# Attention and a soft mixture of experts: score slots of PSUM that share a bank, or have banks of their own

## The chip, the cores and the metric

The kernel runs on one core of one Trainium2 chip. The metric is the device time of one execution in microseconds (us), as the median over several runs. TensorE (PE in the profile) multiplies matrices into PSUM, a memory of 8 banks; a bank holds 512 float32 columns on each of 128 partitions. VectorE (DVE) and ScalarE (ACT) read PSUM, GpSimd (POOL) works on the other on-chip memory alone, and SyncE (SP) issues most DMAs.

## What is computed

Four batches of 12288 queries attend to 768 pooled keys, which are values at the same time. The rows that come out go through a soft mixture of 8 experts with 4 slots each, whose dispatch weights are normalised over all 49152 rows.

```python
kv_pool = kv.reshape(B, H // 4, 4, W // 4, 4, C).mean(axis=(2, 4))
k = v = kv_pool.reshape(B, -1, C) @ w_sr
a = softmax(q @ k.T / sqrt(C))        # 768 keys
x = (a @ v).reshape(B * N, C)
logits = x @ phi                      # 32 slots
d = softmax(logits, axis=0)           # over all rows
slot_out = experts(d.T @ x)           # 8 experts, 4 slots each
return softmax(logits, axis=1) @ slot_out
```

## The kernel before, in words

The attention's output x is never formed. With P the exponentials of a tile of 128 queries, the kernel forms the logits as P times (v phi), and D^T x as (D^T P) v, D being the dispatch weights of the tile.

There are 384 tiles, 12 to a group, 8 groups to a batch, 32 groups in all. For a tile t, the steps and their names in the plan are: `s` (line 384, `qk`), six matmuls that write 768 scores: query high part times key high part (L395), times key low part (L396), query low part times key high part (L397), for each of two pieces; `m` (L401 and L402, VectorE), the row maximum; `e` (L410, ScalarE), the exponential, which frees the scores. For a pair of tiles: `hi` (L417, ScalarE) and `lo` (L421, GpSimd, one per tile), which split half of P into two float16 parts, `pd` (L430, SyncE), a DMA that transposes them, and `tr` (L434, VectorE), which transposes the other half in blocks. There are two buffers for the split parts, so `hi` of a pair waits for the transposes of the pair two before.

For a group, once its 12 tiles are done: `LA` (L464) and `LB` (L476), the logit sums, 48 and 36 matmuls in the program, into four banks; `lev0` and `lev1` (L484 ScalarE, L486 VectorE), which evict two banks each; `lsel` (L492) and `ltr` (L501 to L504), a small product and a transpose; `mmm` and `mred` (L532, L537), which find the running maximum of the logits; `dsub`, `dexp`, `dmul` (L553, L569, L577), which give D; `T0` to `T5` (L592), the product D^T P, 16 matmuls for a pair of tiles; `tacc` (L603), which adds it to `acc`. All of this belongs to the group before, and stands between the score tiles of the next one. For a batch, the keys are formed by `kv_ops`: `kmm` (L277), `khi` (L280) and `klo` (L284), the high and the low part, `umm` (L292), `umax` (L299), `usc` (L308), and the values `vmm`, `vout`.

PSUM is one tile `m` of 8 banks, divided by hand. Score slot A is columns 0 to 767 (bank 0 and half of bank 1), B is 768 to 1535 (the other half of bank 1, and bank 2), C is 1536 to 2303 (bank 3 and half of bank 4). `PIECES` cuts each at the bank's edge, so a slot has one piece of 512 and one of 256 columns, slot B the 256 first. Which tile of a group has which slot stands in `SLOTS`. The logit sums take banks 5, 6, 3 and 4, hence slot C. Small products use bank 5 (sometimes 6), D^T P bank 7, the key products slot C's banks.

Two things set the order. `TAU` gives each step of a group a place, in tiles; `Plan.emit` sorts by it and by what a step depends on, and each engine runs its instructions in this order. The framework then adds waits: where two engines touch the same bank of the tile `m`, the one that is emitted later waits for the one emitted earlier, whichever columns they use.

Of the kernel before, what the change touches and what calls it, by code (L numbers as in the profile page):

```python
# [19 lines left out]
P = 128  # L20
# [3 lines left out]
SLOTS = "ACBACBAABACB"  # L24
# [38 lines left out]
    "T5": 33.921, "dal": 34.589, "tacc": 35.172, "bev": 36.507, "crec28": 37.068, "csub": 38.581, "bacc": 38.859,  # L63
# [33 lines left out]
def attention_then_soft_moe(ctx: ExitStack, tc: tile.TileContext, E, qT, kv0, kvT, w_sr, w_srT, phi, w1, w2, outT, spill):  # L97
# [32 lines left out]
    gp = es.enter_context(tc.tile_pool(name="gp", bufs=3))  # L130
    pm = es.enter_context(tc.tile_pool(name="pm", bufs=1, space=PSUM))

    CAP = {
        "sA": 1, "sB": 1, "sC": 1, "T": 1, "m0": 1, "m1": 1, "p": 13, "pa": 3, "pb": 3, "hl": 2, "q": 3, "qs": 2, "lps": 1, "g": 3,
        "kv": 2, "K": 2, "V": 1, "c": 16, "o0": 1, "o1": 1, "o2": 1, "o3": 1,
# [42 lines left out]
    mt = pm.tile([P, 8, 512], F32, tag="m", name="m")  # L178
    mf = mt.rearrange("p a n -> p (a n)")
    PIECES = {"A": (0, 512, 768), "B": (768, 1024, 1536), "C": (1536, 2048, 2304)}  # L180
    PAIRS = [slice(0, 2), slice(3, 5), slice(6, 8), slice(2, 6, 3)]

    def ss():
        return mt[:, 3:5, :]

    def xs():
        return mt[:, 5, :]

    def slot(t):
        return SLOTS[t % G]  # L190

# [864 lines left out]
```

## Time and profile before

| | us |
|---|---|
| median of 3 runs | 1192.13 (1189.96 to 1200.83) |
| the profiled execution | 1203.68 |
| its span, first to last instruction | 1201.8 |
| TensorE busy | 919.6 (77%) |
| VectorE busy | 786.6 (65%) |
| ScalarE busy | 656.3 (55%) |
| GpSimd busy | 644.2 (54%) |

The first logit sums start at 75.78 us, the last at 1069.59; between them lie 31 periods of a group. In the first 75 us the first batch's keys are loaded, pooled and multiplied; in the last 132 us the experts are computed and 32 blocks of output are written. In the rows of an engine in order of time, the number in brackets at the end is the idle time of that engine just before the instruction, and what ended it.

### The profile page before, as it was taken

What the parts mean: (1) busy time and instruction counts of PE and PEld (TensorE: products, weight loads), DVE (VectorE), ACT (ScalarE), POOL (GpSimd) and SP (SyncE); (2) the same over time, 40 slices, a digit from 0 to 9 for tenths busy, and PEclk for the clock granted to TensorE, in tenths of its full rate; (3) what the DMA queues carried; (4) which work ended last, traced back from release to release, by engine and by line L of the source; (5) the groups of instructions that cost most, each with busy time, mean ns of one, the idle gap of its engine ahead of it and who ended that gap; (6) DMA issues with size and microseconds to landing.
All of it is one profiled execution on the core that took longest, in us unless ns stands there. A gap on an engine that the chain in (4) does not pass through costs nothing. (4 is left out here: it accounts for less than half of the span.)

```text
span 1201.8 us, 26910 instructions
## 1 busy us (share of the span) xinstructions
PE 919.6 (77%) x10436; PEld 605.2 (50%) x10436; DVE 786.6 (65%) x1496; ACT 656.3 (55%) x1244; POOL 644.2 (54%) x774
## 2 busy tenths in 40 slices
PE   2676888878877888788868878887888888876674
PEld 1544555555545555555545555555555555543342
DVE  5464667767765667676756666677666776754764
ACT  1554556666545656666546656665556665631232
POOL 0354556665645666665565656665555665655500
PEclk9788999999998999999989999999999999987755
DMA  7369666867597767766596776675545555575586
GB/s 275 73 122 128 124 133 122 140 128 139 108 119 138 124 136 137 136 118 137 119 128 128 130 130 125 125 119 93 99 90 99 104 105 104 90 211 240 220 355 265
DMA packets 335264, 168.78 MB, mean 140 GB/s; under 512 B 310432, under 2 KB 312736, under 8 KB 335008
## 3 DMA queue, kind: packets, MB, share of 16 engines
q1 hardware_dynamic: 331248, 149.22, 56.5%
q0 software_dynamic: 3456, 17.70, 9.8%
q8 instruction: 82, 1.34, 0.5%
q14 instruction: 46, 0.38, 0.1%
q10 hardware_dynamic: 432, 0.15, 0.0%
HBM read 62.01 MB, written 28.31 MB: 75 GB/s over the span
## 5 line engine op out<-in xcount | busy, mean ns | idle before, releaser
L401 DVE TENSOR_REDUCE nm<-m 128x1 f32<-128x768 f32 x384 | 366.4, 954 | 316.1 <-PE m L397 281.8
L410 ACT ACTIVATE p<-m,nm 128x768 f32<-128x768 f32 x384 | 344.2, 899 | 357.4 <-DVE nm L401 185.1
L421 POOL TENSOR_TENSOR hl<-p,hl 128x384 f16<-128x384 f32 x384 | 346.9, 922 | 287.6 <-ACT hl L417 217.9
L395 PE MATMUL m<-khi,qhi 128*128 128x512 f32 (+1 forms) x768 | 298.8, 389 | 134.9 <-ACT p L410 128.8
L396 PE MATMUL m<-klo,qhi 128*128 128x512 f32 (+1 forms) x768 | 271.0, 353 | 0.0
L397 PE MATMUL m<-khi,qlo 128*128 128x512 f32 (+1 forms) x768 | 270.6, 352 | 0.0
L395 PEld LDWEIGHTS m<-khi,qhi 128*128 128x128 f32 x768 | 152.1, 198 | 228.2 <-ACT p L410 166.6
L592 PE MATMUL m<-p,D 128*32 128x192 f32 x3072 | 166.8, 338 | 44.2 <-DVE acc L603 35.7
L378 POOL TENSOR_TENSOR qlo<-q,qhi 128x512 fp32r<-128x512 f32 x96 | 123.0, 1282 | 129.5 <-ACT qhi L374 126.8
L434 DVE STREAM_TRANSPOSE pa<-p 128x768 f32<-128x768 f32 x192 | 179.1, 958 | 0.0
L417 ACT ACTIVATE hl<-p 128x768 f16<-128x768 f32 x192 | 160.6, 836 | 30.0 <-DMA pb<-hl 30.0
L397 PEld LDWEIGHTS m<-khi,qlo 128*128 128x128 f32 x768 | 153.5, 200 | 18.0
L396 PEld LDWEIGHTS m<-klo,qhi 128*128 128x128 f32 x768 | 153.9, 200 | 14.7 <-issue 0.2
L592 PEld LDWEIGHTS m<-p,D 128*32 128x32 f32 x3072 | 88.2, 112 | 105.6 <-issue 79.5
L464 PE MATMUL m<-pa,vu 32*32 32x384 f32 x3072 | 91.9, 509 | 2.5 <-DVE pa L434 2.5
L410 ACT ACTIVATION_READ_ACCUMULATOR p<-m,nm 128x1 f32 x384 | 74.9, 195 | 0.0
L986 PE MATMUL m<-ct,sl 32*128 32x384 f32 x256 | 51.7, 845 | 24.2 <-DVE ct L980 23.7
L402 DVE TENSOR_SCALAR nm<-nm 128x1 f32<-128x1 f32 x384 | 59.1, 154 | 13.3
L476 PE MATMUL m<-pb,vb 128*32 128x384 f16 x1152 | 54.2, 333 | 10.6 <-DMA pb<-hl 8.1
L464 PEld LDWEIGHTS m<-pa,vu 32*32 32x32 f32 x3072 | 46.3, 105 | 30.1 <-issue 11.0
L374 ACT ACTIVATE qhi<-q 128x512 fp32r<-128x512 f32 x96 | 59.7, 621 | 1.7 <-PE m L396 1.4
L994 ACT ACTIVATE o<-m 128x768 f32<-128x768 f32 x32 | 24.5, 808 | 51.9 <-PE m L986 28.9
(118 smaller groups left out, 693.8 us busy)
## 6 DMA issues: line engine op xcount, KB each, us to landing
q<-qT SPq DMA_DIRECT2D x96, 256.0 KB, 2.7
outT<-o SPq DMA_DIRECT2D x32, 768.0 KB, 4.3
LL<-kvT POOLq DMA_DIRECT2D x21, 768.0 KB, 8.2
raw<-kv SPq DMA_DIRECT2D x8, 768.0 KB, 9.6
pb<-hl SPq DMA_TRANSPOSE x384, 2.8
w_p<-w SPq DMA_DIRECT2D x6, 768.0 KB, 6.6
pa<-w SPq DMA_DIRECT2D x1, 3328.0 KB, 14.3
spill<-LL SPq DMA_DIRECT2D x16, 192.0 KB, 2.1
```

The lines of the kernel that those rows point to most:

```text
L374: nc.scalar.activation(qsp[i][0], src, AF.Copy)
L378: nc.gpsimd.tensor_tensor(out=lo, in0=src, in1=hi.bitcast(F32), op=ALU.subtract)
L395: nc.tensor.matmul(s, hi[:, qc], khi[:, k], start=True, stop=False)
L396: nc.tensor.matmul(s, hi[:, qc], klo[:, k], start=False, stop=False)
L397: nc.tensor.matmul(s, lo[:, qc], khi[:, k], start=False, stop=True)
L401: nc.vector.tensor_reduce(out=NM[t], in_=S[t], axis=X, op=ALU.max, negate=True)
L410: nc.scalar.activation(PP[t // 2][:, t % 2, :], S.pop(t), AF.Exp, bias=NM.pop(t), scale=1.0, accum_out=R[g][:, o : o + 1],)
L417: nc.scalar.activation(HL[k][:, :, 0, :], PP[k][:, :, KA:], AF.Copy)
L421: nc.gpsimd.tensor_tensor(out=hl[:, 1, :], in0=PP[t // 2][:, t % 2, KA:], in1=hl[:, 0, :], op=ALU.subtract)
L434: nc.vector.transpose(out=PA[:, n, :, o : o + 2, :].rearrange("p n a i -> p a n i"), in_=PP[k][:, :, :KA].rearrange("p a (n j) -> p a n j" ...
L464: nc.tensor.matmul(lp(g, c, r), VU[b][rows, kb, :], PA[rows, halves(g), kb, :, :], start=(k == 0), stop=False, skip_group_check=True)
L592: nc.tensor.matmul(d["pst"][c * Q32 : (c + 1) * Q32, :KW], d["D"][:, t, :], pp[:, u, c * KW : (c + 1) * KW], start=(t == 0), stop=(t == G ...
```

## The change

PSUM is allocated anew. A pool `ps` holds three slots of two banks each, taken strictly in turn; a tile of scores takes one and uses 384 columns in each of its two banks. The logit sums of a group take two of these slots (`lq`), one evicted by VectorE, one by ScalarE. The key products, which used slot C's banks, and the products of the experts at the end take slots of the same ring. A tile `m` of two banks is left: bank 0 of it for all small products, bank 1 for D^T P. The six matmuls of a tile write 384 columns each. The maximum and the exponential read two runs of 384. `SLOTS`, `PIECES` and `PAIRS` go, and the table `TAU` is another one, of which two lines are shown.

```diff
-SLOTS = "ACBACBAABACB"
...
-    "s2": -0.107, "m1": -0.08, "e0": 0.0, "ceps11": 0.495, "e1": 0.588, "s3": 0.879, "m2": 0.962, "ceps4": 1.068,
+    "m1": 0.268, "s2": 0.323, "ceps4": 0.44, "ceps0": 0.521, "s3": 0.871, "e1": 0.965, "m2": 0.986, "m3": 1.534,
...
+    ps = es.enter_context(tc.tile_pool(name="ps", bufs=3, space=PSUM))
...
-        "sA": 1, "sB": 1, "sC": 1, "T": 1, "m0": 1, "m1": 1, "p": 13, "pa": 3, "pb": 3, "hl": 2, "q": 3, "qs": 2, "lps": 1, "g": 3,
-        "kv": 2, "K": 2, "V": 1, "c": 16, "o0": 1, "o1": 1, "o2": 1, "o3": 1,
+        "s": 3, "T": 1, "x": 1, "p": 13, "pa": 3, "pb": 3, "hl": 2, "q": 3, "qs": 2, "lps": 1, "g": 3,
+        "kv": 2, "K": 2, "V": 1, "c": 16, "o": 1,
...
-    mt = pm.tile([P, 8, 512], F32, tag="m", name="m")
-    mf = mt.rearrange("p a n -> p (a n)")
-    PIECES = {"A": (0, 512, 768), "B": (768, 1024, 1536), "C": (1536, 2048, 2304)}
-    PAIRS = [slice(0, 2), slice(3, 5), slice(6, 8), slice(2, 6, 3)]
-
-    def ss():
-        return mt[:, 3:5, :]
+    mt = pm.tile([P, 2, 512], F32, tag="m", name="m")
+
+    def ss(name):
+        return ring(ps, "s", [P, 2, 512], name)
 
     def xs():
-        return mt[:, 5, :]
+        return mt[:, 0, :]
...
-            D["pk", b] = ss()
+            D["pk", b] = ss(f"pk_{b}")
...
-        c0, c1, c2 = PIECES[slot(t)]
-        S[t] = mf[:, c0:c2]
-        for a, e in ((c0, c1), (c1, c2)):
-            k = slice(a - c0, e - c0)
-            s = mf[:, a:e]
+        S[t] = ss(f"s_{t}")
+        for h in range(2):
+            k = slice(h * HK, (h + 1) * HK)
+            s = S[t][:, h, :HK]
...
-        nc.vector.tensor_reduce(out=NM[t], in_=S[t], axis=X, op=ALU.max, negate=True)
+        nc.vector.tensor_reduce(out=NM[t], in_=S[t][:, :, :HK], axis=XY, op=ALU.max, negate=True)
...
-            PP[t // 2][:, t % 2, :], S.pop(t), AF.Exp,
+            PP[t // 2][:, t % 2, :].rearrange("p (h n) -> p h n", h=2), S.pop(t)[:, :, :HK], AF.Exp,
...
-            GD[g]["lp"] = [mt[:, k, :LW] for k in (5, 6, 3, 4)]
+            d = GD[g]
+            d["lq"] = [ss(f"lq_{g}_{u}") for u in range(2)]
+            d["lp"] = [d["lq"][r // 2][:, r % 2, :LW] for r in range(NQD)]
...
-        if u == 0:
-            nc.scalar.activation(d["lps"][:, 2:, :], ss()[:, :, :LW], AF.Copy)
+        dst, src = d["lps"][:, 2 * u : 2 * u + 2, :], d["lq"][u][:, :, :LW]
+        if u:
+            nc.scalar.activation(dst, src, AF.Copy)
         else:
-            nc.vector.tensor_copy(d["lps"][:, :2, :], mt[:, 5:7, :LW])
+            nc.vector.tensor_copy(dst, src)
...
-            d["pst"] = mt[:, 7, :]
+            d["pst"] = mt[:, 1, :]
```

Three places of the program where instructions move follow. In these rows a number behind a name tells one tile from another, `nm_146` is the row maximum of score tile 146, and what stands behind "waits" are the semaphores of the engines that the instruction waits for.

The first is ScalarE's queue before, around the exponentials of score tiles 145 to 149, the second to the sixth of group 12; `hl` is the conversion `hi`, `p` the exponentials.

```order
L410 ACTIVATE p_72_4276,r_12_4275<-m_96,nm_145_4272 128x768 [waits DVE_49]
L417 ACTIVATE hl_71_4300<-p_71_4212 128x2x384 [waits DMAHW0_49,DMAHW7_49,Activation_49,Pool_49]
L410 ACTIVATE p_73_4312,r_12_4275<-m_96,nm_146_4297 128x768 [waits DVE_49,PE_49]
L410 ACTIVATE p_73_4312,r_12_4275<-m_96,nm_147_4309 128x768 [waits DVE_49]
L410 ACTIVATE p_74_4338,r_12_4275<-m_96,nm_148_4323 128x768 [waits DVE_49,PE_49]
L417 ACTIVATE hl_72_4341<-p_72_4276 128x2x384 [waits DMAHW2_49,DMAHW3_49,Activation_49,Pool_49]
L410 ACTIVATE p_74_4338,r_12_4275<-m_96,nm_149_4349 128x768 [waits DVE_49,PE_49]
```

The same place now; line 403 is the exponential, line 410 the conversion.

```order
L403 ACTIVATE p_72_4449,r_12_4448<-s_145_4426,nm_145_4452 128x768 [waits DVE_49,PE_49]
L403 ACTIVATE p_73_4492,r_12_4448<-s_146_4456,nm_146_4475 128x768 [waits DVE_49,PE_49]
L410 ACTIVATE hl_72_4507<-p_72_4449 128x2x384 [waits DMAHW2_49,DMAHW3_49,Activation_49,Pool_49]
L403 ACTIVATE p_73_4492,r_12_4448<-s_147_4465,nm_147_4488 128x768 [waits DVE_49,PE_49]
L403 ACTIVATE p_74_4535,r_12_4448<-s_148_4494,nm_148_4517 128x768 [waits DVE_49,PE_49]
L403 ACTIVATE p_74_4535,r_12_4448<-s_149_4510,nm_149_4530 128x768 [waits DVE_49,PE_49]
```

The conversion of pair 72 moved from behind tile 148 to behind tile 146, and each exponential reads a tile of its own (`s_146`) in place of a part of the one tile `m`.

The second place is TensorE's queue before, at the start of the logit sums of group 11 (`pa` and `vu` are their operands), behind the last score tile that is issued ahead of them.

```order
L395 MATMUL m_96<-khi_1_2685,qhi_37_4238 128x256
L396 MATMUL m_96<-klo_1_2686,qhi_37_4238 128x256
L397 MATMUL m_96<-khi_1_2685,qlo_37_4239 128x256
L464 MATMUL m_96<-pa_91,vu_1_3056 32x384 [waits DVE_49]
L464 MATMUL m_96<-pa_91,vu_1_3056 32x384 x7
L464 MATMUL m_96<-pa_91,vu_1_3056 32x384 [waits Activation_49]
L464 MATMUL m_96<-pa_91,vu_1_3056 32x384 x39
```

The same place now, with the pieces of D^T P (line 588) that stand ahead of it.

```order
L588 MATMUL m_99<-p_62_3778,D_10_4399 32x192 x8
L588 MATMUL m_99<-p_63_3863,D_10_4399 32x192 x8
L388 MATMUL s_150_4548<-khi_1_2894,qhi_37_4435 128x384 [waits Activation_49]
L389 MATMUL s_150_4548<-klo_1_2895,qhi_37_4435 128x384
L390 MATMUL s_150_4548<-khi_1_2894,qlo_37_4436 128x384
L459 MATMUL lq_11_0_4560<-pa_94,vu_1_2913 32x384 [waits DVE_49,Activation_49]
L459 MATMUL lq_11_0_4560<-pa_94,vu_1_2913 32x384 x7
L459 MATMUL lq_11_1_4561<-pa_94,vu_1_2913 32x384 [waits Activation_49]
L459 MATMUL lq_11_1_4561<-pa_94,vu_1_2913 32x384 x7
```

The piece for pair 63 stood behind the sums and stands ahead of them now, and the sums wait for two exponentials (one for each slot that they take) in place of one.

The third place is TensorE's queue before, at the end of a batch, from the small product `lsel` of group 14 on: the key products of batch 2 (line 277), and four score tiles of batch 1 still to come behind them.

```order
L492 MATMUL m_96<-lps_14_5416,selb_1_3039 32x384 [waits Activation_49]
L592 MATMUL m_96<-p_81_4767,D_13_5277 32x192 x8
L277 MATMUL m_96<-LL_90,w_sb_70 128x384 [waits DMASW7_49,DMASW6_49]
L277 MATMUL m_96<-LL_90,w_sb_70 128x384
L395 MATMUL m_96<-khi_1_2685,qhi_47_5472 128x512 [waits Activation_49]
L396 MATMUL m_96<-klo_1_2686,qhi_47_5472 128x512
```

The key products now (lines 271 and 286), with the first score tile of the next batch, `s_192`, behind them.

```order
L271 MATMUL pk_2_5898<-LL_93,w_sb_73 128x384 [waits DMASW7_49,DMASW6_49,Activation_49]
L286 MATMUL pu_2_5900<-LL_93,wp4_92 128x384 [waits Activation_49]
L286 MATMUL pu_2_5900<-LL_93,wp4_92 128x384
L271 MATMUL pk_2_5898<-LL_93,w_sb_73 128x384 [waits Activation_49]
L588 MATMUL m_99<-p_84_5185,D_14_5872 32x192 [waits DVE_49,Pool_49]
L588 MATMUL m_99<-p_84_5185,D_14_5872 32x192 x7
L588 MATMUL m_99<-p_85_5228,D_14_5872 32x192 x8
L388 MATMUL s_192_5943<-khi_2_5896,qhi_48_5791 128x384 [waits PE_49]
L389 MATMUL s_192_5943<-klo_2_5897,qhi_48_5791 128x384 [waits DVE_49]
```

The key products moved from four tiles ahead of the batch's end to its end, with D^T P of two pairs of tiles (84 and 85) between them and the first tile that reads the new keys.

## Rows read from the trace of the kernel before

**Rows 1.** Busy time of PE, PEld, DVE, ACT, POOL; clock, DMA share, GB/s.

```profile
470.23:500.45 30.22, 24.65 (x311) 16.46 (x310) 21.42 (x40) 19.17 (x37) 19.26 (x23) 1.00 0.80 142
75.78:1069.59 993.81, 795.92 (x9656) 532.95 (x9655) 674.20 (x1276) 597.62 (x1146) 584.03 (x675) 0.96 0.67 121
```

**Rows 2.** TensorE in order of time: start, duration, instruction, [idle before, released by].

```profile
474.96 0.50 PE L395 MATMUL m<-khi,qhi 128*128 128x512 f32 x1 [0.38 <-ACT p L410]
...
479.02 0.50 PE L395 MATMUL m<-khi,qhi 128*128 128x512 f32 x1 [0.27 <-ACT p L410]
...
483.93 0.39 PE L395 MATMUL m<-khi,qhi 128*128 128x256 f32 x1 [1.04 <-ACT p L410]
...
489.86 0.86 PE L592 MATMUL m<-p,D 128*32 128x192 f32 x16 [1.54 <-DVE acc L603]
490.67 0.39 PE L395 MATMUL m<-khi,qhi 128*128 128x256 f32 x1
...
492.70 0.50 PE L395 MATMUL m<-khi,qhi 128*128 128x512 f32 x1
...
493.74 0.28 PE L397 MATMUL m<-khi,qlo 128*128 128x256 f32 x1
493.85 0.39 PE L395 MATMUL m<-khi,qhi 128*128 128x512 f32 x1
...
498.16 0.38 PE L395 MATMUL m<-khi,qhi 128*128 128x256 f32 x1 [2.31 <-ACT p L410]
...
500.45 0.93 PE L464 MATMUL m<-pa,vu 32*32 32x384 f32 x32
```

**Rows 3.** VectorE in the same group, in order of time.

```profile
487.39 0.96 DVE L401 TENSOR_REDUCE nm<-m 128x1 f32<-128x768 f32 x1 [2.94 <-PE m L397]
...
494.12 0.96 DVE L401 TENSOR_REDUCE nm<-m 128x1 f32<-128x768 f32 x1 [1.38 <-PE m L397]
...
495.19 0.95 DVE L401 TENSOR_REDUCE nm<-m 128x1 f32<-128x768 f32 x1
```

**Rows 4.** ScalarE in the same group, in order of time.

```profile
475.54 0.81 ACT L484 ACTIVATE lps<-m 128x768 f32<-128x768 f32 x1
...
496.23 0.90 ACT L410 ACTIVATE p<-m,nm 128x768 f32<-128x768 f32 x1 [2.29 <-DVE nm L401]
...
497.12 0.89 ACT L410 ACTIVATE p<-m,nm 128x768 f32<-128x768 f32 x1
```

**Rows 5.** Groups of instructions: busy us, mean ns of one, idle us before, releasers.

```profile
L421 POOL TENSOR_TENSOR hl<-p,hl 128x384 f16<-128x384 f32 x384 | 346.9, 922 | 287.6 <-ACT hl L417 217.9 <-issue 58.2 <-POOL hl L421 11.2
...
L417 ACT ACTIVATE hl<-p 128x768 f16<-128x768 f32 x192 | 160.6, 836 | 30.0 <-DMA pb<-hl 30.0
...
L284 DVE SCALAR_TENSOR_TENSOR klo<-m,khi 128x384 fp32r<-128x384 f32 x8 | 4.5, 557 | 2.1 <-ACT khi L280 1.8
L280 ACT ACTIVATE khi<-m 128x384 fp32r<-128x384 f32 x8 | 3.9, 492 | 14.5 <-PE m L277 14.5
...
L299 DVE TENSOR_REDUCE am<-m 128x1 f32<-128x768 f32 x4 | 3.6, 911 | 1.6 <-PE m L292 1.6
```

**Rows 6.** Waits of the whole span: us in total, times, longest us.

```profile
ACT p L410 <- DVE nm L401: 185.1, 63, 4.9
...
ACT hl L417 <- DMA pb<-hl: 30.0, 10, 9.8
```

**Rows 7.** DMA issues: kind, count, median us from issue to landing.

```profile
pb<-hl SPq DMA_TRANSPOSE x384, 2.8
```

**Rows 8.** Busy times as in rows 1, at the change to batch 2.

```profile
626.20:630.40 4.20, 4.20 (x16) 3.34 (x12) 1.68 (x3) 0.63 (x1) 3.39 (x4) 0.50 0.72 141
```

**Rows 9.** TensorE there, in order of time.

```profile
625.27 1.08 PE L642 MATMUL m<-v,aT 96*32 96x128 f32 x16 [5.22 <-ACT aT L635]
626.28 0.80 PE L395 MATMUL m<-khi,qhi 128*128 128x512 f32 x1
...
628.37 0.63 PE L395 MATMUL m<-khi,qhi 128*128 128x512 f32 x1
```

More of the change, by code (lines that the diff above doesn't have):

```diff
@@ L23 @@
 Q32 = 32
-SLOTS = "ACBACBAABACB"
 TAU = {
[29 rows of a table removed]
-    "xso19": 18.569, "xho13": 18.628, "lsel": 18.723, "reps": 18.763, "csum5": 18.808, "rinv": 19.089, "ltr": 19.295,
-    "ln": 19.621, "ceps0": 19.702, "mcol": 20.139, "kv2": 20.444, "cmul26": 20.596, "ceps9": 20.963, "mmm": 21.149,
-    "mred": 21.593, "dsub": 21.833, "dexp": 22.394, "dmul": 22.795, "xh6": 23.132, "T0": 23.466, "ceps12": 23.982,
[3 rows of a table removed]
-    "T5": 33.921, "dal": 34.589, "tacc": 35.172, "bev": 36.507, "crec28": 37.068, "csub": 38.581, "bacc": 38.859,
[13 rows of a table removed]
[29 rows of a table added]
+    "lev0": 18.513, "lev1": 18.513, "crec11": 18.527, "reps": 18.807, "rinv": 18.974, "lsel": 19.037, "ltr": 19.601,
+    "ln": 20.079, "csum19": 20.551, "csum25": 20.707, "mcol": 21.235, "mmm": 21.629, "mred": 22.122, "dsub": 22.358,
[5 rows of a table added]
+    "kv4": 39.365, "cmul27": 40.126, "bev": 40.196, "uhl": 42.368, "cexp": 43.449, "spill": 44.522, "wl4": 44.887,
[12 rows of a table added]
 }
@@ L176, in ring @@
         return pool.tile(shape, dt, tag=tag, name=name, bufs=CAP[ringname or tag])
-    mt = pm.tile([P, 8, 512], F32, tag="m", name="m")
-    mf = mt.rearrange("p a n -> p (a n)")
-    PIECES = {"A": (0, 512, 768), "B": (768, 1024, 1536), "C": (1536, 2048, 2304)}
-    PAIRS = [slice(0, 2), slice(3, 5), slice(6, 8), slice(2, 6, 3)]
-    def ss():
-        return mt[:, 3:5, :]
+    mt = pm.tile([P, 2, 512], F32, tag="m", name="m")
+    def ss(name):
+        return ring(ps, "s", [P, 2, 512], name)
     def xs():
-        return mt[:, 5, :]
-    def slot(t):
-        return SLOTS[t % G]
+        return mt[:, 0, :]
     last = {}
@@ L202, in w_mm @@
     def w_mm():
-        D["pw"] = mt[:, 6, :]
+        D["pw"] = mt[:, 0, :]
         nc.tensor.matmul(D["pw"][:, :NS], wT_sb, phi_sb, start=True, stop=True)
@@ L209, in w_out @@
         )
-    a = op("PE", "hw", -90, [], w_mm, acq=[("m1", "pw")])
-    ops_w = op("ACT", "hwo", -90, [a], w_out, use=[("m1", "pw")])
+    a = op("PE", "hw", -90, [], w_mm, acq=[("x", "pw")])
+    ops_w = op("ACT", "hwo", -90, [a], w_out, use=[("x", "pw")])
     raw = {}
@@ L289, in u_mm @@
     def u_mm(b):
-        D["pu", b] = ss()
+        D["pu", b] = ss(f"pu_{b}")
         for h in range(2):
@@ L318, in u_t @@
     def u_t(b):
-        D["put", b] = ss()[:, 0, :]
+        D["put", b] = ss(f"put_{b}")[:, 0, :]
         for k in range(NBB):
@@ L333, in v_mm @@
             V96[b] = ring(bp, "v96", [P, 2 * NQD, C], f"v96_{b}", F32, "V")
-            D["pv", b] = ss()
+            D["pv", b] = ss(f"pv_{b}")
         for k in range(NQD):
@@ L345, in kv_ops @@
         for h in range(2):
-            m = ("sC", ("pk", b))
+            m = ("s", ("pk", b))
             a = op("PE", f"{pre}kmm{h}", at, dep[h] + ([ops["km", b]] if h else []), lambda h=h: k_mm(b, h), acq=[m, ("K", b)] if h == 0 else [], use=po + [m])
@@ L350, in kv_ops @@
             ops["k", b, h] = op("DVE", f"{pre}klo{h}", at, [a], lambda h=h: k_lo(b, h), use=[m])
-        m = ("sC", ("pu", b))
+        m = ("s", ("pu", b))
         us = ("lps", ("us", b))
-        pt = ("sC", ("put", b))
+        pt = ("s", ("put", b))
         a = op("PE", pre + "umm", at, dep[0] + dep[1] + [ops_w], lambda: u_mm(b), acq=[m], use=po + [("K", b)])
@@ L361, in kv_ops @@
         for h in range(2):
-            m = ("sC", ("pv", b))
+            m = ("s", ("pv", b))
             a = op("PE", f"{pre}vmm{h}", at, dep[0] + dep[1] + ([ops["vm", b]] if h else []), lambda h=h: v_mm(b, h), acq=[m, ("V", b)] if h == 0 else [], use=po + [m, ("V", b)])
@@ L685, in plan_tile @@
             need.append(ops["T", (k - CAP["p"]) // GP])
-        ops["s", t] = op("PE", f"s{og}", at, need, lambda: qk(t), acq=[("s" + slot(t), t)], use=[("qs", i), ("K", b)])
-        ops["m", t] = op("DVE", f"m{og}", at, [ops["s", t]], lambda: rmax(t), use=[("s" + slot(t), t)])
+        ops["s", t] = op("PE", f"s{og}", at, need, lambda: qk(t), acq=[("s", t)], use=[("qs", i), ("K", b)])
+        ops["m", t] = op("DVE", f"m{og}", at, [ops["s", t]], lambda: rmax(t), use=[("s", t)])
         ops["e", t] = op(
             "ACT", f"e{og}", at, [ops["m", t]] + ([ops["e", t - 1]] if t else []), lambda: pexp(t),
-            acq=([("p", k)] if u == 0 else []) + ([("g", g)] if og == 0 else []), use=[("s" + slot(t), t), ("p", k), ("g", g)],
+            acq=([("p", k)] if u == 0 else []) + ([("g", g)] if og == 0 else []), use=[("s", t), ("p", k), ("g", g)],
         )
@@ L712, in plan_logits @@
         at = g * G
-        sl = [("m0", ("L", g)), ("m1", ("L", g)), ("sC", ("L", g))]
+        sl = [("s", ("L", g, 0)), ("s", ("L", g, 1))]
         t = g * G + G - 1
@@ L725, in plan_logits @@
         ops["lb", g] = a
-        e0 = op("ACT", "lev0", at, [a], lambda: l_ev(g, 0), use=[sl[2]] + lk)
-        e1 = op("DVE", "lev1", at, [a], lambda: l_ev(g, 1), use=sl[:2] + lk)
-        mk = ("m0", ("psl", g))
+        e0 = op("ACT", "lev0", at, [a], lambda: l_ev(g, 1), use=[sl[1]] + lk)
+        e1 = op("DVE", "lev1", at, [a], lambda: l_ev(g, 0), use=[sl[0]] + lk)
+        mk = ("x", ("psl", g))
         a = op("PE", "lsel", at, [e0, e1, ops["us", b]], lambda: l_sel(g), acq=[mk], use=lk + [("K", b)])
@@ L740, in plan_group @@
         a = op("DVE", "mcol", at, [ln], lambda: m_col(g), use=gk)
-        mk = ("m0", ("pg", g))
+        mk = ("x", ("pg", g))
         a = op("PE", "mmm", at, [a], lambda: m_mm(g), acq=[mk], use=gk)
@@ L770, in plan_batch @@
         at = g * G
-        m1, m2 = ("m0", ("pa", b)), ("m0", ("pb", b))
+        m1, m2 = ("x", ("pa", b)), ("x", ("pb", b))
         a = op("PE", "btr", at, [ops["ta", g]], lambda: b_tr(b), acq=[m1])
@@ L862, in e_h @@
         if k0 == 0:
-            W["ph", h] = mt[:, (3, 7)[h], :]
+            W["ph", h] = ss(f"ph_{h}")[:, 0, :]
         for k in range(k0, k0 + NQD):
@@ L875, in e_ht @@
             W["hT"] = cp.tile([P, NF, NS], F32, tag="hT", name="hT")
-        pht = W["pht", h] = mt[:, (6, 0)[h], :]
+        pht = W["pht", h] = ss(f"pht_{h}")[:, 0, :]
         for f in range(HF):
@@ L886, in e_o @@
         if f0 == 0:
-            W["pso", h] = mt[:, (3, 7)[h], :]
+            W["pso", h] = ss(f"pso_{h}")[:, 0, :]
         for f in range(f0, f0 + HF):
@@ L918, in tail @@
         return op(eng, f"{kind}{n_[0]}", DRAIN, deps, fn, acq=acq, use=use)
-    a = tail("PE", "xpsi", [ops["b", B - 1]], e_psi, acq=[("m0", "psi")])
-    s0 = tail("DVE", "xsm", [a], lambda: e_sm(0), use=[("m0", "psi")])
-    s1 = tail("DVE", "xsm", [a], lambda: e_sm(1), use=[("m0", "psi")])
-    tot = tail("DVE", "xtot", [a], e_tot, use=[("m0", "psi")])
+    a = tail("PE", "xpsi", [ops["b", B - 1]], e_psi, acq=[("x", "psi")])
+    s0 = tail("DVE", "xsm", [a], lambda: e_sm(0), use=[("x", "psi")])
+    s1 = tail("DVE", "xsm", [a], lambda: e_sm(1), use=[("x", "psi")])
+    tot = tail("DVE", "xtot", [a], e_tot, use=[("x", "psi")])
     hh, hx = [], []
     for h in range(2):
-        k = (("sC", "T")[h], ("ph", h))
+        k = ("s", ("ph", h))
         a = tail("PE", "xh", [s0] + wl[1] + hx[-1:], lambda h=h: e_h(h, 0), acq=[k], use=wuse[1])
@@ L932, in attention_then_soft_moe @@
     for h in range(2):
-        k = (("m1", "sA")[h], ("pht", h))
+        k = ("s", ("pht", h))
         a = tail("PE", "xht", [hh[h]], lambda h=h: e_ht(h), acq=[k], use=[("lps", "hs")])
@@ L939, in attention_then_soft_moe @@
     for h in range(2):
-        k = (("sC", "T")[h], ("pso", h))
+        k = ("s", ("pso", h))
         a = tail("PE", "xo", ho[:2] + wl[2] + ([a] if a else []), lambda h=h: e_o(h, 0), acq=[k], use=wuse[2])
@@ L943, in attention_then_soft_moe @@
         sq.append(tail("DVE", "xso", [a] + sq, lambda h=h: e_so(h), use=[k]))
-    a = tail("PE", "xq", sq[1:], e_q, acq=[("m0", "psq")])
-    fin = tail("ACT", "xfin", [a, tot], e_fin, use=[("m0", "psq")])
+    a = tail("PE", "xq", sq[1:], e_q, acq=[("x", "psq")])
+    fin = tail("ACT", "xfin", [a, tot], e_fin, use=[("x", "psq")])
     def rm(g):
@@ L982, in o_mm @@
     def o_mm(k, u):
-        po = U[k, u] = mt[:, PAIRS[pairs[k][u]], :]
+        po = U[k, u] = mt if pairs[k][u] == 3 else ss(f"po_{k}_{u}")
         for r in range(2):
@@ L1011, in attention_then_soft_moe @@
         for u in range(2):
-            sk = (f"o{pairs[k][u]}", k)
+            sk = ("o" if pairs[k][u] == 3 else "s", ("po", k, u))
             a = op("PE", f"omm{u}", at, [a, fin], lambda k=k, u=u: o_mm(k, u), acq=[sk], use=[ck])
```

89 rows, old and new, of the table TAU are left out of this document.

## The prediction

> **What bounds the kernel now.** I read the busy time by stretch first. Over the loop, from the first logit sums at 75.78 us to the last at 1069.59, 31 group periods, TensorE is busy for 80% of the time (795.92 of 993.81 us), VectorE 68%, ScalarE 60%, GpSimd 59%, the DMA engines 67% [rows 1]: nothing is full. So the loop is held by waits between engines, and the next thing to read is one clean group from one logit sum to the next, in order of time, on each engine.
>
> The group from 470.23 to 500.45 us lasts 30.22 us; TensorE is busy 24.65 us of it at the full clock level, VectorE 21.42, ScalarE 19.17, GpSimd 19.26 [rows 1]. TensorE's missing 5.57 us are nearly all in five waits [rows 2]: 0.38, 0.27, 1.04, 1.54 and 2.31 us, together 5.54 us.
>
> The next step is why each ends so late, and it is the shared bank 1, which holds 256 columns of slot A and 256 of slot B. Take the tile in slot B that starts at 490.67 [rows 2]. Its last matmul is issued about 1.1 us later, but its row maximum starts only at 494.12, after 1.38 us of idle VectorE [rows 3]. What ended just before is not its own matmul but the second piece of the next tile in slot A (L397 at 493.74 + 0.28 = 494.02, rows 2), which writes bank 1. The maximum is done some 1.1 us later, but the exponential of this tile starts at 496.23, behind 2.29 us of idle ScalarE, released by L401, the maximum of the A tile (495.19 + 0.95 = 496.14) [rows 3, 4]: again bank 1. The next tile in slot B then waits for the A tile's exponential (497.12 + 0.89 = 498.01) and starts at 498.16, 2.31 us late [rows 2, 4]. The 1.04 us wait at 483.93 also stands before a 256-column first piece, slot B's form. The 1.54 us one is indirect: D^T P of the new group waits for the addition to `acc` (L603), which stands in VectorE's queue behind a maximum that waited 2.94 us for TensorE (487.39), once more a B tile, the one from 483.93, held until the following A tile had written bank 1 [rows 2, 3]. The pair occurs two times a group: 63 waits of an exponential for the maximum of another tile, 185.1 us of idle ScalarE [rows 6].
>
> So of 5.54 us, 4.89 (1.04 + 1.54 + 2.31) come from the shared bank and 0.65 (0.38 + 0.27) are slots that were in use for their own sake.
>
> **The change part by part.** *Separate banks.* Every tile gets two banks of its own, so a maximum waits for its own scores only, an exponential for its own maximum, and a matmul for the exponential that last used its slot. That removes the 4.89 us. The work does not change: six matmuls a tile, 384 + 384 columns in place of 512 + 256. The maximum and the exponential now read two runs of 384; the row that has that form on this chip is the maximum of the pooled logits, L299, 911 ns [rows 5] against 0.96 us for the plain form [rows 3]: I cost the new form at nothing.
>
> *Three slots for everything.* Scores, the two halves of the logit sums and the key products now take turns in three slots. Between the logit sums' start and their eviction two of three are taken: from 470.23 to 475.54 + 0.81 in the trace [rows 2, 4], some 6.1 us, during which before had two score slots left and now one has. The new order fits this: before the sums TensorE issues one score tile more and both D^T P pieces, and during the sums VectorE has three transposes and one maximum, ScalarE one exponential and one conversion. TensorE itself issues no score during the sums, before or after. The sums wait for two exponentials at their start; a slot's shortest round is 1.15 (six matmuls, 492.70 to 493.85, rows 2) + 1.1 (maximum, 494.12 to 495.19, rows 3) + 0.9 (exponential, rows 4) + an estimated 0.45 of hand-over, 3.6 us, while one tile comes every 2.1 us and there are three slots. I take 0 for this, with 0 to 2 us a group as the range.
>
> *One tile of two banks for small products and D^T P.* The order shows D^T P waiting for VectorE after the small products have been read, which it did not before. By then the reader has run; I take 0.
>
> *Keys of the next batch* are formed later: before four score tiles ahead of the batch's end, now right in front of the first tile that needs them. The high part takes 0.492 and the low part 0.557 us [rows 5]; with the product before them and the hand-overs I estimate 2 us, then the pipeline fills again (a round, 3.6 us), with 1.6 us of D^T P beside it. I take 5 us for each of three changes of batch, 15 us; the range is 0 to 10 each.
>
> *Denser DMA.* Conversions (L417) wait for the transposes two pairs back: 30.0 us in 10 waits now [rows 6]. The chain of a conversion (0.836), two subtractions (0.922 each) and a landing (2.8) [rows 5, 7] is 5.5 us, without the issue and the hand-overs; two pairs have a third of a group for it, 10 us now and 8.4 after, so a late landing is felt sooner. I add half of the 30.0 us again, 15 us; the range is 0 to 60.
>
> *Sum.* A clean group: 24.65 + 0.65 = 25.30 us, 4.92 less than 30.22. The mean period is 993.81 / 31 = 32.06, 1.84 over a clean one (changes of batch, late DMAs), which I leave as it is. So 31 x 4.92 = 152.5 us less, 15 and 15 us more: 122.5 us less. The stretch before the first sums (75.78 us) and behind the last (1201.8 - 1069.59 = 132 us, bound by the output DMAs and a chain of small steps) keep their order in the main, so 0 there, 10 us either way. Against the profiled execution's 1203.68 us that is 1081.2; the median of the runs, 1192.13, is 0.9904 of it, which gives 1071 us.
>
> *A rule that speaks against it.* The clock is at its full level (1.00, 2.4 GHz) through the clean group in spite of waits of 2.31 us [rows 1, 2]; it is seen at 0.50 (1.2 GHz) at 626.20, behind a wait of 5.2 us for ScalarE at a change of batch [rows 8, 9]. The Trainium skill, TensorE: Matmul & The Clock Gate, section "A second HAM failure mode: psum-queue depth-cycling", tells of a kernel that cycles through PSUM banks each iteration, idles shortly between groups of matmuls and so swings between the two clock levels. By that rule a ring of three slots taken in turn would be worse than the three fixed ones; by the rows shorter idles leave the clock where it is. The sum goes by the rows; the rule is a rival below.
>
> **The rivals.**
> *The DMA engines become the bound.* They are busy 0.80 of the clean group, 24.2 us [rows 1]. If they cannot pass 0.90, 24 groups (those with loads for the next batch) stop at 26.9 us: 38 us on top, 1109. If they cannot pass 0.80, these gain nothing, 118 us on top: 1188. In the middle 1145. For it: landings wait in one queue. Against it: the whole loop has 0.67, and the last batch has no such loads.
>
> *The ring of slots becomes the bound* (the slower side). Fourteen holds a group share three slots, the two of the sums 6 us each. If a score holds its slot h us, the group lasts (12 h + 12) / 3. Now h is 496.23 + 0.90 - 490.67 = 6.5 in slot B and 498.01 - 492.70 = 5.3 in slot A [rows 2, 4]. It decides from h = 5.3 on, and the kernel is slower than before from about 6.6. With 6.8 the group takes 31.2 us, 5.9 over the forecast: 1252 us. For it: one late exponential holds up a ring that is taken strictly in turn. Against it: the 6.5 contains the bank waits, without which 3.6 to 5 us are left.
>
> *The change does not do what it says.* If two banks of one tile still count as one, D^T P waits for the small products: up to 2 us a group, 62 us, 1132.
>
> *The clock falls.* At the low level a score tile takes 628.37 - 626.28 = 2.09 us [rows 9] against 1.15. With 4 of 12 tiles at that level, 3.8 us a group: 1187 us.
>
> **How the numbers follow.** The forecast, 1071 us, with its own range of 1035 to 1110: 0.68. DMA bound 0.12, ring bound 0.07, banks still shared 0.06, clock 0.05, the rest 0.02. The low end of the range is TensorE's busy time alone (31 x 0.65 = 20 us less), no cost at changes of batch and no DMA term (30 less): 1022, say 1025; the high end is 1150, which takes in the DMA case's middle and the shared banks. A measurement tells about 1% here. Faster by over 1%: forecast, most of DMA and shared banks, half of the clock, 0.88. Within 1%: 0.05. Slower: 0.07.
>
> **What would show it.** In the profile after: a clean group of 25 to 26 us from sum to sum; no wait of an exponential for the maximum of another tile; no 256-column form, and TensorE's waits before L388 released by ScalarE, short; D^T P's first piece without the 1.54 us; TensorE at 95% in the clean stretches. Waits of L410's conversion for the transposes show the DMA case, scores that wait for exponentials of three tiles before in every group the ring. The prediction is wrong if the clean group stays over 28 us though the bank waits are gone.

## The result and the profile after

| | before | after |
|---|---|---|
| median of 4 runs, us | 1192.32 (1189.96 to 1200.83) | 1023.92 (1019.80 to 1028.77) |
| the profiled execution | 1203.68 | 1019.80 |
| its span | 1201.8 | 1018.0 |
| ratio after / before | | 0.858, 95% interval 0.852 to 0.864 |

The profiled execution before was slower than all four timed ones, so the profiled executions lie 183.9 us apart and the medians 168.4. The change makes the kernel 14% faster. The forecast was 1071 us with a range from 1025: the direction and the mechanism hold, the size does not, and the time lies just below the range.

Busy times by stretch, in the columns of [rows 1]: the loop from the first logit sums to the last, one clean group, the stretch before the loop and the one behind it.

```profile
62.52:894.80 832.28, 776.29 (x9671) 557.55 (x9671) 673.59 (x1274) 604.74 (x1146) 580.80 (x676) 0.98 0.80 143
827.72:851.65 23.93, 23.83 (x312) 17.50 (x311) 21.82 (x42) 19.93 (x39) 18.26 (x21) 1.00 0.74 134
...
0.00:62.52 62.52, 34.25 (x144) 28.00 (x145) 43.07 (x70) 29.58 (x56) 22.52 (x29) 0.95 0.74 204
894.80:1018.02 123.22, 73.56 (x626) 37.75 (x622) 70.71 (x153) 29.50 (x44) 37.74 (x70) 0.72 0.74 299
```

The clean group lasts 23.93 us in place of 30.22, and TensorE is busy all the time. It is the best case: only six of the 31 periods last at most 24.2 us, five of them from 703 us on, and the others up to 31. The work is the same, so the five waits of [rows 2] should be gone, and TensorE in order of time shows it:

```profile
827.72 2.75 PE L459 MATMUL lq<-pa,vu 32*32 32x384 f32 x96
830.40 1.65 PE L471 MATMUL lq<-pb,vb 128*32 128x384 f16 x36
831.98 0.45 PE L388 MATMUL s<-khi,qhi 128*128 128x384 f32 x1
...
838.98 0.34 PE L390 MATMUL s<-khi,qlo 128*128 128x384 f32 x1
839.15 0.34 PE L388 MATMUL s<-khi,qhi 128*128 128x384 f32 x1
839.33 0.34 PE L389 MATMUL s<-klo,qhi 128*128 128x384 f32 x1
```

No row of this group has a bracket: nothing stops TensorE, not even for a slot. The last rows show something else. A matmul is listed with 0.34 us, and the next one starts 0.17 us later.

VectorE and ScalarE around one tile of the same group, as in [rows 3, 4] (`nm` the maximum, `p` the exponential):

```profile
836.43 0.95 DVE L394 TENSOR_REDUCE nm<-s 128x1 f32<-128x768 f32 x1
837.42 0.15 DVE L395 TENSOR_SCALAR nm<-nm 128x1 f32<-128x1 f32 x1
```

```profile
837.66 0.90 ACT L403 ACTIVATE p<-s,nm 128x768 f32<-128x768 f32 x1
```

The exponential starts right behind its own maximum. In the waits of the whole span, exponentials are released by L395, the last step of their own maximum; there is no row any more in which one waits for L394, as 63 did for L401 [rows 6]. But the conversion's wait for transposes has tripled from 30.0 us:

```profile
ACT hl L410 <- DMA pb<-hl: 92.4, 39, 5.7
ACT p L403 <- DVE nm L395: 83.7, 121, 2.3
```

That is the new bottleneck, and the place around 600 us shows it whole. First GpSimd's load of pooled keys, then a transpose in the queue of SyncE (SPq) with its time from issue to landing, and the median of all transposes beside it, then ScalarE, then TensorE:

```profile
591.27 0.88 POOL L259 DMA_DIRECT2D LL<-kvT  x1
```

```profile
592.00 1.26 SPq L423 DMA_TRANSPOSE pb<-hl  x1
```

```profile
pb<-hl SPq DMA_TRANSPOSE x1, 9.0
```

```profile
pb<-hl SPq DMA_TRANSPOSE x384, 3.2
```

```profile
601.15 0.84 ACT L410 ACTIVATE hl<-p 128x768 f16<-128x768 f32 x1 [5.50 <-DMA pb<-hl]
601.90 0.79 ACT L480 ACTIVATE lps<-lq 128x768 f32<-128x768 f32 x1
```

```profile
602.75 1.49 PE L488 MATMUL m<-lps,selb 128*32 128x384 f32 x4 [3.27 <-ACT lps L480]
604.17 0.69 PE L388 MATMUL s<-khi,qhi 128*128 128x384 f32 x1
```

A load of 768 KB starts. The transpose issued 0.7 us behind it lands 9.0 us after its issue, at 601.0, where the median is 3.2. The conversion waits 5.50 us for it; behind it on ScalarE stands the eviction of the logit sums, and for that TensorE waits 3.27 us. The granted clock (the seventh number of a window) falls with the stop and is back after 608:

```profile
600.00:602.00 2.00, 0.00 (x0) 0.00 (x0) 0.00 (x0) 0.85 (x2) 0.00 (x0) 0.86 0.66 150
...
604.00:606.00 2.00, 2.00 (x8) 1.83 (x7) 0.99 (x4) 1.37 (x3) 2.00 (x3) 0.50 0.74 145
606.00:608.00 2.00, 2.00 (x8) 2.00 (x7) 1.11 (x2) 0.73 (x2) 1.56 (x3) 0.50 0.72 179
608.00:612.00 4.00, 3.92 (x34) 3.23 (x33) 3.40 (x10) 2.99 (x6) 0.47 (x2) 0.97 0.51 102
```

This group lasts 30.58 us instead of 23.93.

### The profile page after: what moved, and what is told of

It reads as the page before. It is cut to its first block, busy times and chain, and to the rows that moved or that the text cites. A ratio compares the mean times of both kernels' runs of the same rounds, so it can differ in the third digit from the quotient of the medians.

```text
span 1018.0 us, 27047 instructions
## 1 busy us (share of the span) xinstructions
PE 884.1 (87%) x10436; PEld 623.3 (61%) x10436; DVE 787.4 (77%) x1496; ACT 663.8 (65%) x1244; POOL 641.1 (63%) x774
## 5 line engine op out<-in xcount | busy, mean ns | idle before, releaser
L394 DVE TENSOR_REDUCE nm<-s 128x1 f32<-128x768 f32 x384 | 363.3, 946 | 68.9 <-PE s L390 66.4
L403 ACT ACTIVATE p<-s,nm 128x768 f32<-128x768 f32 x384 | 344.0, 896 | 91.3 <-DVE nm L395 83.7
L388 PE MATMUL s<-khi,qhi 128*128 128x384 f32 x768 | 287.6, 374 | 21.8 <-ACT p L403 21.7
L389 PE MATMUL s<-klo,qhi 128*128 128x384 f32 x768 | 263.4, 343 | 2.1 <-DVE klo L278 2.1
L390 PE MATMUL s<-khi,qlo 128*128 128x384 f32 x768 | 263.8, 343 | 0.0
L410 ACT ACTIVATE hl<-p 128x768 f16<-128x768 f32 x192 | 161.2, 840 | 98.9 <-DMA pb<-hl 92.4
L388 PEld LDWEIGHTS s<-khi,qhi 128*128 128x128 f32 x768 | 148.5, 193 | 92.7 <-issue 46.6
L389 PEld LDWEIGHTS s<-klo,qhi 128*128 128x128 f32 x768 | 149.0, 194 | 3.3 <-DVE klo L278 3.0
L390 PEld LDWEIGHTS s<-khi,qlo 128*128 128x128 f32 x768 | 148.0, 193 | 0.0
L459 PE MATMUL lq<-pa,vu 32*32 32x384 f32 x3072 | 88.6, 492 | 1.5 <-DVE pa L427 1.5
L403 ACT ACTIVATION_READ_ACCUMULATOR p<-s,nm 128x1 f32 x384 | 74.1, 193 | 0.0
L395 DVE TENSOR_SCALAR nm<-nm 128x1 f32<-128x1 f32 x384 | 59.1, 154 | 13.2
```

What stands on the lines that cost most here:

```text
L388: nc.tensor.matmul(s, hi[:, qc], khi[:, k], start=True, stop=False)
L389: nc.tensor.matmul(s, hi[:, qc], klo[:, k], start=False, stop=False)
L390: nc.tensor.matmul(s, lo[:, qc], khi[:, k], start=False, stop=True)
L394: nc.vector.tensor_reduce(out=NM[t], in_=S[t][:, :, :HK], axis=XY, op=ALU.max, negate=True)
L403: nc.scalar.activation(PP[t // 2][:, t % 2, :].rearrange("p (h n) -> p h n", h=2), S.pop(t)[:, :, :HK], AF.Exp, bias=NM.pop(t), scale=1.0, ...
L410: nc.scalar.activation(HL[k][:, :, 0, :], PP[k][:, :, KA:], AF.Copy)
```

## The experiments

All ratios are to the kernel before, run beside each. Four corners first: banks and order apart.

**Own banks, old order.** The changed kernel with the old `TAU`, all of the table.

```diff
-    "m1": 0.268, "s2": 0.323, ...
+    "s2": -0.107, "m1": -0.08, ...
```

> The changed kernel with the old table of places: two banks for every score slot, the order of the kernel before. Theory (the shared bank made the gain): no exponential waits for the maximum of another tile any more, a clean group lasts 24 to 26.5 us instead of 30.22, the stretch ahead of the first logit sums shrinks from 75.8 to 62 to 66 us, the total is 1020 to 1065 us. Rival (the new order made it): without the new places the clean group stays at 28 us or more and the total at 1120 us or more.

Measured: 1091.39 us, ratio 0.914 (0.908 to 0.921). No exponential waits for another tile's maximum, and a clean group takes 25.39 us, as the theory said; the stretch ahead of the loop takes 57.6, less than it said, and the total lies between what the two theories allowed. So the banks alone give some 102 us of the 168 (8.6% against 14.2%): the order is a second cause, not the first. TensorE in such a group has two stops:

```profile
896.98:922.37 25.39, 24.66 (x312) 17.59 (x311) 21.89 (x43) 19.50 (x38) 18.28 (x21) 1.00 0.74 133
```

```profile
896.98 0.87 PE L459 MATMUL lq<-pa,vu 32*32 32x384 f32 x16
898.31 2.63 PE L459 MATMUL lq<-pa,vu 32*32 32x384 f32 x80 [0.46 <-ACT p L403]
900.88 1.65 PE L471 MATMUL lq<-pb,vb 128*32 128x384 f16 x36
...
911.05 0.86 PE L588 MATMUL m<-p,D 128*32 128x192 f32 x16 [0.27 <-DVE gm L533]
```

In the old order the sums wait for their second slot, and D^T P for the maximum of the logits (`gm`). The sums' bracket shows 0.46 us, but from the sums' start to their second part 3.90 us pass (900.88 - 896.98) against 2.68 after the full change (830.40 - 827.72).

**Shared banks, new order.** The kernel before with the new `TAU`. Its plan does not hold the slots of the key products apart, and in this order `umm` (L292) writes over the first key product in slot C before `khi` (L280) has read it, as TensorE and ScalarE show at a change of batch:

```profile
569.03 1.65 PE L277 MATMUL m<-LL,w_sb 128*128 128x384 f32 x2
570.47 1.59 PE L292 MATMUL m<-LL,wp 128*128 128x384 f32 x4
```

```profile
571.45 0.49 ACT L280 ACTIVATE khi<-m 128x384 fp32r<-128x384 f32 x1 [0.92 <-PE m L292]
```

So the keys that this kernel forms are not the right ones. The score tiles and the sums use their slots in turn, and the work is the same.

> The kernel before with the new table of places: score slots A and B share bank 1 as before. Theory (the shared bank): the waits of exponentials for the next tile's maximum stay, some 60 of them or more with 150 us in total, a clean group stays at 29 us or more, the total is 1150 to 1250 us. Rival (the new order made the gain): the clean group falls below 27 us and the total below 1100 us.

Measured: 1229.23 us, ratio 1.031 (1.026 to 1.036). A clean group takes 31.03 us, and the exponentials' waits for the next tile's maximum grow from 185.1:

```profile
ACT p L410 <- DVE nm L401: 249.9, 86, 4.6
```

The theory holds: without banks of its own the new order is a loss, with them it is worth another 67 us.

**Pieces of 512 and 256 in own banks.**

```diff
-        for h in range(2):
-            k = slice(h * HK, (h + 1) * HK)
-            s = S[t][:, h, :HK]
+        sf = S[t].rearrange("p a n -> p (a n)")
+        for k in (slice(0, 512), slice(512, 768)):
+            s = sf[:, k]
...
```

The maximum and the exponential read one run of 768 columns again, too.

> The changed kernel with the matmuls of a score tile cut at 512 and 256 columns, as before, in the two banks that the tile has for itself. Theory (TensorE's busy time in a clean group fell from 24.65 to 23.83 us because it no longer stops, not because of the cut): the clean group stays within 0.2 us of 23.93, the total within 1% of 1024 us. Rival (equal pieces make TensorE faster): 0.7 us a group come back, 22 us in all, about 1046 us.

Measured: 1025.54 us, ratio 0.862 (0.856 to 0.868), a clean group 24.03 us with TensorE busy 23.93. The cut is worth nothing, and TensorE's busy time fell for another reason: the group has no stop.

**One tile, own banks.** The slots cut by hand out of one tile.

```diff
-    ps = es.enter_context(tc.tile_pool(name="ps", bufs=3, space=PSUM))
...
-    mt = pm.tile([P, 2, 512], F32, tag="m", name="m")
+    mt = pm.tile([P, 8, 512], F32, tag="m", name="m")
+    turn = iter(range(10**6))
     def ss(name):
-        return ring(ps, "s", [P, 2, 512], name)
+        k = 2 + 2 * (next(turn) % 3)
+        return mt[:, k : k + 2, :]
...
```

> The changed kernel with its three slots, the small products and D^T P cut by hand out of one tile of 8 banks, as in the kernel before, each with the same banks for itself. Theory (what counts is the bank, not the tile it belongs to): within 1% of 1024 us, a clean group of 23.9 to 24.2 us, no exponential that waits for another tile's maximum. Rival (parts of one tile hold each other up whatever banks they have, and the pool of three separate tiles made the gain): 1080 us or more.

Measured: 1031.22 us (1017.56 to 1035.92), within 1% of the changed kernel, clean groups of 23.99 to 24.30 us, and no exponential waits for another tile's maximum. The bank decides, not the tile.

**Three buffers for the split halves.** What is left over a clean group.

```diff
-        ... "hl": 2, ...
+        ... "hl": 3, ...
```

> The changed kernel with three buffers for the split halves in place of two, so that a conversion waits for the transposes of three pairs back. Theory (what is left over a clean group, 2.92 us a period or 90 us, is mostly late transposes that hold the conversion, 92.4 us in 39 waits, and the low clock behind such a stop): these waits fall below 30 us, the total to 970 to 1000 us. Rival (the transposes' data itself is late, so the logit sums wait for it instead): no more than 10 us are gained, 1012 to 1025 us.

Measured: 971.93 us, ratio 0.813 (0.808 to 0.819), a clear gain over the change's 0.858. The loop, and the conversions' waits:

```profile
59.76:842.79 783.03, 756.08 (x9671) 548.25 (x9672) 673.87 (x1274) 608.01 (x1146) 581.21 (x677) 0.99 0.87 152
```

```profile
ACT hl L410 <- DMA pb<-hl: 12.3, 8, 4.6
```

The loop is 49 us shorter (832.28 - 783.03), and 20 of its 31 periods last at most 24.2 us, in place of six. The theory holds.

**The same in the kernel before.**

> The kernel before, banks shared and old order, with three buffers for the split halves. Theory (late transposes were mostly covered by the bank waits there, 30.0 us of waiting conversions in all): 5 to 30 us are gained, 1162 to 1188 us. Rival (a third buffer is worth the same everywhere, some 52 us as on the changed kernel): about 1142 us.

Measured: 1185.13 us, ratio 0.9995 (0.995 to 1.004), no gain where the theory expected one. Its loop, and two of its waits:

```profile
72.69:1067.97 995.28, 796.78 (x9657) 532.99 (x9656) 674.85 (x1276) 597.20 (x1146) 583.27 (x674) 0.97 0.69 120
```

```profile
ACT hl L417 <- DMA pb<-hl: 7.3, 3, 4.4
```

```profile
PE m L476 <- DMA pb<-hl: 22.3, 7, 6.9
```

The latter in the kernel before with two buffers:

```profile
PE m L476 <- DMA pb<-hl: 8.1, 5, 2.4
```

The loop is as long as before (993.81 us). The conversions' waits fall from 30.0 to 7.3 us, but the logit sums' waits for transposes (L476) grow from 8.1 to 22.3: here the buffer only moves the wait. That the bank waits cover late transposes, as the theory has it, this doesn't show.

**Fewer loads, two buffers.** Six of eight loads of pooled keys left out per batch (the expectation says which).

```diff
-        for c in range(1, R2 // KVC):
+        for c in range(1, 2):
```

> The changed kernel with six of the eight loads of each next batch's pooled keys left out (the first two and the fold stay, so the pooled keys are a partial sum; all else is computed as before). Theory (the loads delay the transposes, and these hold the conversions): of 92.4 us of conversions waiting for transposes about a third is left, 20 to 40 us, and the total is 978 to 1000 us. Rival (the transposes are late because there are more of them per us now, with or without loads): waits of 60 us or more, 1008 us or more.

Measured: 960.60 us, ratio 0.810 (0.806 to 0.814), better than the theory's range; the waits lie in theirs.

```profile
ACT hl L410 <- DMA pb<-hl: 25.8, 19, 4.9
```

It is the loads that make the transposes late, not the transposes' own number.

**Loads moved, with two buffers and with three.**

The entries of the table, gathered from several lines:

```diff
-"kv1": 8.274, "kv2": 15.539, "kv3": 25.517, "kv4": 39.365, "kv5": 51.744, "kv6": 68.759, "kv7": 78.841, "kf0": 86.106
+"kv1": 6.6, "kv2": 16.5, "kv3": 28.5, "kv4": 40.5, "kv5": 52.5, "kv6": 64.5, "kv7": 76.5, "kf0": 88.5
```

> The changed kernel with its two buffers, and the loads of the next batch's pooled keys at another place of the group (6.6, 16.5, 28.5 and so on to 88.5 tiles in the table, so 4.5 tiles behind a group's start from the second on, after its last transposes are issued). Theory (a load delays whatever transposes are issued in its 8 us, and two buffers can't hold that anywhere in the group): conversions still wait 50 to 100 us in all, 1000 to 1030 us. Rival (only the place of the loads matters): below 985 us.

Measured: 1051.73 us, ratio 0.884 (0.878 to 0.890), slower than both theories said; the conversions wait 112.4 us in 35 waits, more than either. Place does matter, the other way: with two buffers this one is worse.

> The changed kernel with three buffers and the loads moved as in the kernel with two. Theory (with three buffers what is left of the late transposes are waits of the logit sums' second part for the group's last ones, 2 to 4.4 us at six groups): these waits are below 1 us now, the total 945 to 965 us. Rival (the delay only moves to other transposes): 968 to 985 us.

Measured: 965.80 us, ratio 0.812 (0.805 to 0.819): not told apart from 0.813 without the move, though the conversions' waits fall from 12.3 to 4.6 us and the sums' waits for transposes from 13.7 to 3.7. Inconclusive between the theories.

**Old order, own banks, three buffers.**

> The changed kernel's banks with the old order, and three buffers for the split halves (1091 us with two). Theory (in the old order the sums wait for two slots, so a clean group takes 25.4 us against 23.9: 45 us in all, whatever the buffers): 1020 to 1050 us. Rival (the old order lost only to late transposes): below 1000 us.

Measured: 1071.71 us, ratio 0.900 (0.894 to 0.907), above both ranges. The buffer gives 20 us here, 52 in the new order. A clean group stays at 25.35 us, and the late transposes are met one step further, by the second part of the logit sums:

```profile
PE lq L471 <- DMA pb<-hl: 39.4, 15, 5.9
```

The new order has 13.7 us there with three buffers. That its table puts more room between a group's last transposes and this step (`pd11` 14.25, `LB0` 17.563, against 14.88 and 16.756) would explain it; no run changed that alone.

**Keys formed early, three buffers.**

```diff
-    ... "kmm0": 95.812, "umm": 95.812, ...
+    ... "kmm0": 91.0, "umm": 91.0, ...
```

> Three buffers, and the products of the next batch's keys (kmm0 and umm in the table) at 91.0 tiles in place of 95.8, some four tiles ahead of the batch's end as in the kernel before. With three buffers and the late keys 971.9 us were measured. Theory (keys formed late cost TensorE 1.2 us of waiting at each of three changes, as the trace shows: 0.54 us for the product's own slot and 0.69 us for the low part): the waits for the low part go, the total stays within 8 us, 964 to 980 us. Rival (5 us at each change, as the prediction had it): 952 to 960 us.

Measured: 987.68 us, ratio 0.827 (0.823 to 0.832), slower than with the late keys (0.813), against both. TensorE at the first change of batch:

```profile
225.89 0.45 PE L388 MATMUL s<-khi,qhi 128*128 128x384 f32 x1 [1.78 <-ACT us L302]
228.56 0.44 PE L388 MATMUL s<-khi,qhi 128*128 128x384 f32 x1 [1.36 <-ACT p L403]
230.37 0.69 PE L388 MATMUL s<-khi,qhi 128*128 128x384 f32 x1 [0.49 <-ACT p L403]
```

The waits for the low part are gone, but early key products hold slots of the ring in the middle of the scores, which then wait 3.6 us here (again at the second change; 3.1 in two waits at the third). Here late is the better place. The waits at the three changes explain about 7 of the 16 us (10.4 against 3.6); the rest stays unexplained: the first change also has a 5.9 us wait of the sums for transposes, ahead of these rows.

## Why the prediction missed, point by point

In the terms of the sum, on the profiled executions (-122.5 us forecast, -183.8 measured):

| term | forecast | measured |
|---|---|---|
| clean group, 31 x | -4.92 each, -152.5 | -6.29 each, -195.0 |
| over a clean group, 57.0 before | +30 | +33.5 |
| ahead of the first sums | 0 | -13.3 |
| behind the last sums | 0 | -9.0 |

(57.0 is 993.81 - 31 x 30.22; after it is 832.28 - 31 x 23.93 = 90.5.) Of the 61.3 us between the sums, 14 don't show in the medians: I scaled by 0.9904, and the profiled run after lies below its median.

*The mechanism is right.* The waits of rows 2 to 4 went with the shared bank. (One reading of them is loose, and nothing hangs on it: the last matmul of the B tile at 490.67 starts 0.92 us behind the first, at 491.59, not 1.1.) Banks alone take the clean group to 25.39 us, and the form in two runs costs nothing: 946 ns a maximum (L394), as in the kernel that reads one run of 768 from its own banks. The Trainium skill, PSUM — Partial Sum Buffer, section "PSUM bank collisions raise a hardware error", says to guard PSUM by bank (and quadrant), not by address, since no two engines may be on one bank at once. The traces agree as far as the framework's waits go: slots that only touched in one bank waited for each other, and did not when each had banks of its own. What the chip does without these waits no run here shows.

*The step that failed is the sum's "A clean group: 24.65 + 0.65 = 25.30 us".* It took TensorE's busy time as a floor and carried the two slot waits over; the group came out 1.37 us shorter, 42.5 of the 61.3 us. Neither part is fixed. The busy time fell to 23.83 with the same matmuls, and the run with the old pieces (23.93) shows that their cut isn't the reason. A matmul is listed with 0.34 us and the next starts after 0.17, so part of a stop counts as busy: in the corner with own banks and the old order the two brackets hold 0.73 us, but the group is 1.46 us longer than with the new order, and its busy time is 24.66. The Trainium skill, Perfetto Trace Analysis, section "Identifying the Most-Contended Engine", warns that matmul busy time is no measure of how near a kernel is to its limit, because matmuls are pipelined. The traces agree: 24.65 and 23.83 us for the same matmuls. And the two slot waits did not stay: in that corner neither score tile has a bracket any more, the sums and D^T P have the two stops instead, and these went through the new order, which I had credited with fitting the three slots ("I take 0", and a loss as the range), not with a gain: 25.39 us in the old order, 23.93 in the new, 31 x 1.46 = 45 us. The low end of the range stood on the same floor.

*"0 there, 10 us either way" for the ends.* Ahead of the first sums lies the first group, whose tiles had the same waits. TensorE of the kernel before, in this stretch, in front of slot B's form:

```profile
57.75 0.38 PE L395 MATMUL m<-khi,qhi 128*128 128x256 f32 x1 [2.24 <-ACT p L410]
...
63.50 0.39 PE L395 MATMUL m<-khi,qhi 128*128 128x256 f32 x1 [2.34 <-DVE nm L401]
...
71.64 0.58 PE L395 MATMUL m<-khi,qhi 128*128 128x256 f32 x1 [3.08 <-ACT p L410]
```

I counted 31 groups, and the waits [rows 6] were those of 32. The run with own banks in the old order, 57.6 us to the first sums, shows that the banks did it. Behind the last sums the cause of the 9 us is open. The kernel before with three buffers, in the same order, has 123.83 us there at a clock of 0.73, where the first profile had 132.21 at 0.61; so the change isn't needed for it, but the output blocks use these buffers too, and chance and the buffer are not told apart.

*Keys late, +15.* Wrong. The trace has 0.48 to 0.54 us of waiting for the product's slot and 0.69 for the low part at each change, 3.6 us in all, and with three buffers forming them early costs more than it saves.

*Denser DMA, +15.* Right in kind, far too small: the third buffer is worth 49 us of the loop. I took half of 30.0 us again. In the kernel before the third buffer gained nothing; in the new pace a delayed transpose reaches TensorE and takes the clock along.

*"Leave as is" for the rest over a clean group.* It shrank from 57.0 to 41 us without the late transposes (783.03 - 31 x 23.93). In its loop the kernel before waited 8.35 and 5.22 us for `aT` (L642; the second is the one of [rows 9], with the low clock behind it), and after has no such wait there. Both were late transposes already, as ScalarE shows just ahead of the eviction of `aT`:

```profile
362.81 0.84 ACT L417 ACTIVATE hl<-p 128x768 f16<-128x768 f32 x1 [9.82 <-DMA pb<-hl]
...
364.44 0.37 ACT L635 ACTIVATE aT<-m 96x256 f32<-96x256 f32 x1
```

```profile
623.23 0.84 ACT L417 ACTIVATE hl<-p 128x768 f16<-128x768 f32 x1 [6.68 <-DMA pb<-hl]
...
624.85 0.37 ACT L635 ACTIVATE aT<-m 96x256 f32<-96x256 f32 x1
```

So the rest that I left as it is held late transposes too. The misses of the terms over a clean group (keys, DMA, the rest) cancelled almost exactly, and +33.5 near +30 is no confirmation.

*The rivals.* The ring didn't become the bound and the banks do count apart. The clock is 0.98 over the loop, 1.00 in the clean group: three slots in turn did not make it swing. The DMA case is the one with truth in it, but as delay, not as bandwidth: with three buffers the DMA engines' share rises to 0.87 of the loop and the time falls. The middle of that rival is about 1149 us by its own ends, 1109 and 1188, not 1145; neither is near.

## What to carry to other kernels

Before costing a removed wait, work out what an engine needs from the spacing of back-to-back instructions, not from its busy time, and count the waits over the whole program, ends included. Give every buffer that two engines touch banks of its own before tuning the order: here the order was a loss of 3% without them and 67 us of gain with them. When a stall that sets the pace goes, look at what waits behind it: here one more buffer for the transposes gained nothing before and 49 us of the loop after, for 972 us, faster than both kernels.

## What the runs showed of the hardware that was not expected

With a 768 KB load from GpSimd's queue under way, a transpose on another queue landed 9.0 us after its issue, where the median is 3.2, and with six of eight loads 72% of the conversions' waits went (92.4 to 25.8 us). TensorE's clock was 0.50 for 5.4 us behind 3.27 us of idle time (602.75 to 608.18), so this stop, the only one of its group, cost 6.6 us (30.58 against 23.93), twice its length.
